# An RWKV-style recurrence followed by a multiplicative feed-forward: the order of every engine's instructions comes from the kernel's own list schedule

## The chip, the cores and the metric

The kernel runs on one core of one Trainium2 chip. The metric is the device time of one execution in microseconds (us). The time before is the median of three runs, 225.25 us (224.19 to 225.88).

## The reference

For each of 4 batches and 8 heads a state of 48 by 48 runs over 768 steps; the outputs, 3072 tokens of 384, then go through a feed-forward with a product of two projections.

```python
def _attn_ref(r, k, v, w, u):
    ...
    for t in range(S):
        kt, vt, rt, wt = (k[:, :, t], v[:, :, t], r[:, :, t], w[:, :, t])
        cur = np.einsum('bhd,bhe->bhde', u[None] * kt, vt)
        y[:, :, t] = np.einsum('bhd,bhde->bhe', rt, state + cur)
        state = wt[:, :, :, None] * state + np.einsum('bhd,bhe->bhde', kt, vt)
def _moe_ref(x, w1, w2, w3, w_out):
    return ((x @ w1) * (x @ w2) @ w3) @ w_out
```

Shapes: r, k, v, w are 4 x 8 x 768 x 48 float32; w1 and w2 are 384 x 1024, w3 is 1024 x 1024, w_out is 1024 x 384.

## The kernel before

**Units.** The sequence is cut into chunks of 128 steps. A unit is one chunk of one batch with all 8 heads: 24 units, n = 0 to 23, six for each batch, which hand a state on from unit to unit. `load(n)` (L102) issues four transfers on SyncE (SP) for a unit: w, k, r, v, each 128 partitions of eight rows of 192 bytes. Eight units' buffers exist, so `load(n + 8)` stands behind `att(n)` in the program (L304).

**Attention of a unit.** This is a chain that goes back and forth between engines: ScalarE (ACT) takes the logarithm of w (L121); TensorE (PE) forms the cumulative sums `cs` (L145); ACT takes the exponential (L146); VectorE (DVE) multiplies k and r by it into `krt` (L148); PE transposes `krt` in eight steps into `tr` (L152); ACT copies `tr` to `trs` (L155); PE forms the scores `mps` (L185); DVE masks them in two halves, `mbf` (L188); PE forms `y` from the state and the masked scores (L225, L230); DVE adds `yd` (L235); PE transposes the result, `yt` (L238); ACT copies it into the block's `xT` (L243). Beside it PE forms the state's increment `kv` and a column of decays (L194, L198), ACT takes an exponential (`pc`, L202), DVE adds the state (L207) and scales it (L215), and GpSimd (POOL) writes the state as a block-diagonal operand (`sbd`, L211). POOL also casts v (L124) and forms u times k times r (`uk`, L158, L159); DVE reduces that to `dsum` (L167) and POOL multiplies it with v (`yd`, L169).

**Feed-forward.** Units are gathered in blocks of 2, 2, 4, 4, 4, 4, 2, 2. For a block, `ffn_ab` (L249) runs for eight slices of 128 columns: three matmuls with w1 into `a_ps`, three with w2 into `b_ps`, an ACT copy of `a_ps` (L263), a DVE product into `abT` (L264). w3 and w_out are multiplied once into `w34`: `w34_transpose` (L275) transposes w3 in eight groups of eight, `w34_mul` (L281) runs eight groups of eight matmuls into `pm`. `ffn_out` (L266) runs eight matmuls for each unit, an ACT copy, and the store on SP.

**Weights.** `load_w` (L129) issues w1 and w2 on POOL in the middle of unit 1 (L161), w3 and w_out in the middle of unit 3 (L164). POOL issues nothing else of transfers.

**The order.** The program is written as a list of feed-forward parts with a cost in us each (L310 to L328): blocks 0 and 1 of `ffn_ab`, the transposes of w3, the products `w34`, the two blocks of `ffn_out`, then block by block. Before each part, units are emitted as long as `nxt < lead + done / every` with lead 3 and every 4.1 (L330). The framework then puts the instructions of each engine in an order of its own by that program order, by data dependence, by free buffers and by its own durations; only the four weight issues are pinned to their place. Once built, each engine works through its instructions strictly in that order.

Of the kernel before, what the change touches and what calls it, by code (L numbers as in the profile page):

```python
# [7 lines left out]
F32 = mybir.dt.float32  # L8
BF = mybir.dt.bfloat16
Alu = mybir.AluOpType  # L10
Act = mybir.ActivationFunctionType


@with_exitstack
def kernel(
# [26 lines left out]
    NTOK = B * S  # L42
# [17 lines left out]
    ps_ffn = ctx.enter_context(tc.tile_pool(name="ps_ffn", bufs=3, space=bass.MemoryType.PSUM))  # L60
    ps_att = ctx.enter_context(tc.tile_pool(name="ps_att", bufs=2, space=bass.MemoryType.PSUM))
# [30 lines left out]
    for t in lw_st:  # L92
        nc.vector.memset(t.rearrange("p h d -> p (h d)").bitcast(F32), 0.0)
    for t in kr_st:
        nc.vector.memset(t.rearrange("p g h d -> p (g h d)").bitcast(F32), 0.0)
    for t in sb_st:
        nc.vector.memset(t.rearrange("p h d -> p (h d)").bitcast(F32), 0.0)


    ins = {}  # L100

    def load(n):  # L102
        b, c = divmod(n, NC)

        def src(ap):
            return ap[b, :, c * C:(c + 1) * C, :].rearrange("h t d -> t h d")

        w_in = inp.tile([C, H, D], F32, tag="w_in", name="w_in")
        kr_in = inp.tile([C, 2, H, D], F32, tag="kr_in", name="kr_in")
        v_in = inp.tile([C, H, D], F32, tag="v_in", name="v_in")  # L110
        nc.sync.dma_start(w_in, src(w))  # L111
        nc.sync.dma_start(kr_in[:, 0], src(k))  # L112
        nc.sync.dma_start(kr_in[:, 1], src(r))  # L113
        nc.sync.dma_start(v_in, src(v))  # L114
        ins[n] = (w_in, kr_in, v_in)

    vbs = {}

    def prep(n):
        lw = lw_st[n % NS]  # L120
        nc.scalar.activation(lw[:, :, 0:D], ins[n][0], Act.Ln)  # L121
        lws[n] = lw
        v_bf = work.tile([C, H, D], BF, tag="v_bf", bufs=3)
        nc.gpsimd.tensor_copy(v_bf, ins[n][2])  # L124
        vbs[n] = v_bf

    lws = {}

    def load_w(dst, ap):  # L129
        with tc.high_priority():  # L130
            d = nc.gpsimd.dma_start(dst, ap.rearrange("(i p) f -> p i f", p=P))
        tc.keep_in_program_order(d)

    state = {}

    def att_a(n):

        b, c = divmod(n, NC)
        lw = lws[n]
        v_bf = vbs[n]  # L140
        kr_in = ins[n][1]
        e_sb = work.tile([C, 2, H, D], F32, tag="e_sb")
        cs = ps_m.tile([C, 2, TB], F32, tag="m", name="cs")
        for j, lt in enumerate((LTn_incl, LT_strict)):
            nc.tensor.matmul(cs[:, j, 0:DM], lhsT=lt, rhs=lw[:, :, 0:D], start=True, stop=True)  # L145
        nc.scalar.activation(e_sb.rearrange("t j h d -> t j (h d)"), cs[:, :, 0:DM], Act.Exp)  # L146
        krt = kr_st[n % NS]
        nc.vector.tensor_mul(krt[:, :, :, 0:D], kr_in, e_sb)  # L148
        tr = ps_att.tile([C, 2, HP, C], BF, tag="att")
        for j in range(2):  # L150
            for p in range(HP):
                nc.tensor.transpose(tr[:, j, p, :],  # L152
                                    krt[:, j, 2 * p:2 * p + 2, :].rearrange("t h d -> t (h d)"), I128)
        trs = work.tile([C, 2, HP, C], BF, tag="trs")
        nc.scalar.copy(trs, tr)  # L155

        uk = work.tile([C, H, D], F32, tag="uk")
        nc.gpsimd.tensor_mul(uk, kr_in[:, 0], u_bc)  # L158
        nc.gpsimd.tensor_mul(uk, uk, kr_in[:, 1])  # L159
        if n == 1:  # L160
            load_w(w1_bf, moe_w1)  # L161
            load_w(w2_bf, moe_w2)
        if n == 3:
            load_w(w3_bf, moe_w3)  # L164
            load_w(wo_bf, moe_w_out)
        dsum = work.tile([C, H], F32, tag="dsum")
        nc.vector.reduce_sum(dsum, uk, axis=mybir.AxisListType.X)  # L167
        yd = work.tile([C, H, D], BF, tag="yd")
        nc.gpsimd.tensor_mul(yd, v_bf, dsum[:, :, None].to_broadcast([C, H, D]))  # L169
        state[n] = (krt, trs, yd)  # L170

    prev = {}

    def att_b(n):

        b, c = divmod(n, NC)
        lw = lws.pop(n)
        v_bf = vbs.pop(n)
        krt, trs, yd = state.pop(n)
        mbf = work.tile([C, 2, HP, C], BF, tag="mbf")  # L180
        mps = ps_m.tile([C, 2, HP, C], F32, tag="m", name="mps")
        for p in range(HP):
            for q in range(2):
                o = q * DP
                nc.tensor.matmul(mps[:, q, p, :], lhsT=trs[o:o + D, 0, p, :],  # L185
                                 rhs=trs[o:o + D, 1, p, :], start=True, stop=True)
        for q in range(2):
            nc.vector.tensor_mul(mbf[:, q], mps[:, q], mask)  # L188

        if c < NC - 1:  # L190
            kv = ps_att.tile([C, HP, D + 1], F32, tag="att")
# [5 lines left out]
            for p in range(HP):
                nc.tensor.matmul(kv[:, p, D:D + 1],  # L198
                                 lhsT=lw[:, 2 * p:2 * p + 2, :].rearrange("t h d -> t (h d)"),
                                 rhs=ones_c, start=True, stop=True)  # L200
            pc = work.tile([C, HP], F32, tag="pc")
            nc.scalar.activation(pc[:, :, None], kv[:, :, D:D + 1], Act.Exp)  # L202
            ts_ = work.tile([C, HP, D], F32, tag="tsum")
            if c == 0:
                nc.vector.tensor_copy(ts_, kv[:, :, 0:D])
            else:
                nc.vector.tensor_add(ts_, prev[b][0], kv[:, :, 0:D])  # L207
            s_bd = sb_st[n % NS]
            for q in range(2):
                o = q * DP  # L210
                nc.gpsimd.tensor_mul(s_bd[o:o + DP, :, q * D:(q + 1) * D], ts_[o:o + DP],  # L211
                                     pc[o:o + DP, :, None].to_broadcast([DP, HP, D]))
            s_f = work.tile([C, HP, D], F32, tag="s_f")
            if c < NC - 2:
                nc.vector.tensor_mul(s_f, ts_, pc[:, :, None].to_broadcast([C, HP, D]))  # L215
            nxt = (s_f, s_bd)
        else:
            nxt = None

        y = ps_y.tile([C, H, D], F32, tag="y")  # L220
        first = True
        if c > 0:
            s_bd = prev[b][1]
            for p in range(HP):
                nc.tensor.matmul(y[:, 2 * p:2 * p + 2, :], lhsT=trs[:, 1, p, :], rhs=s_bd[:, p, :],  # L225
                                 start=first, stop=False)
                first = False
        for p in range(HP):
            for q in range(2):
                nc.tensor.matmul(y[:, 2 * p + q, :], lhsT=mbf[:, q, p, :], rhs=v_bf[:, 2 * p + q, :],  # L230
                                 start=first, stop=(p == HP - 1 and q == 1))
                first = False
        prev[b] = nxt
        y_bf = work.tile([C, DM], BF, tag="y_bf")
        nc.vector.tensor_add(y_bf.rearrange("t (h e) -> t h e", h=H), y, yd)  # L235
        yt = ps_att.tile([C, DI, C], BF, tag="att")
        for di in range(DI):
            nc.tensor.transpose(yt[:, di, :], y_bf[:, di * P:(di + 1) * P], I128)  # L238
# [127 lines left out]
```

## Time and profile before

| quantity | value |
|---|---|
| median of three runs | 225.25 us (224.19 to 225.88) |
| the profiled execution's own time | 225.09 us |
| its span, first to last instruction | 223.4 us |
| PE busy | 176.8 us, 79% of the span |
| DVE busy | 133.1 us, 60% |
| POOL busy | 115.4 us, 52% |
| ACT busy | 108.9 us, 49% |
| bytes moved | 28.54 MB in 106342 packets, of which 100304 are under 512 bytes |

The span is that of one profiled execution; its time is 1.7 us more than the span, and 0.16 us under the median. "Busy" of PE is the union of its matmuls' records, whose ends are modelled, so that it also holds the last matmul's way through the array ahead of a pause. L numbers are lines of the kernel before. A row of a timeline gives the start, the length of the group, the engine and line, the operation, the number of instructions, and in brackets the idle time of the engine ahead of it with what ended it.

### The profile page before, as it was taken

To read this page: it belongs to the slowest core of one execution; us is meant where nothing else is said; L and a number is where in the kernel's file an instruction comes from. 1 tells how busy PE (TensorE), PEld (TensorE's weight loads), DVE (VectorE), ACT (ScalarE), POOL (GpSimd) and SP (SyncE) were. 2 spreads that over 40 slices of the span, in tenths; PEclk is the share of its full clock that TensorE was granted. 3 is DMA by queue.
4 is the path that set the end of the run, shared out by engine and by line. 5 is a ranking of instruction groups with operands and counts; after the bars stand their busy time and mean duration, and the time that the engine had idled before them with its cause. 6 is when DMAs were issued, how large, how long until landed. Compare 5 with 4: busy or idle time off the path is not lost.

```text
span 223.4 us, 4564 instructions
## 1 busy us (share of the span) xinstructions
PE 176.8 (79%) x1720; PEld 103.5 (46%) x1720; DVE 133.1 (60%) x238; ACT 108.9 (49%) x213; POOL 115.4 (52%) x152
## 2 busy tenths in 40 slices
PE   1044169805898898987899879998999999999993
PEld 0033136603576555553355534455545544557771
DVE  5174055426579964456878458773897657853360
ACT  3222234603462374636565566567566566544441
POOL 4598265136997588767636775767363332100000
PEclk9999999975899999999999999999999999999999
DMA  7999999999999999996449987611000110002101
GB/s 130 197 167 200 202 182 193 199 190 183 195 190 168 195 170 202 177 213 107 109 95 197 203 187 165 113 36 74 35 3 0 72 72 0 3 37 106 38 37 70
DMA packets 106342, 28.54 MB, mean 128 GB/s; under 512 B 100304, under 2 KB 104528, under 8 KB 106320
## 3 DMA queue, kind: packets, MB, share of 16 engines
q1 hardware_dynamic: 103440, 23.80, 58.7%
q0 software_dynamic: 2880, 4.46, 11.4%
q8 instruction: 13, 0.21, 0.4%
q14 instruction: 9, 0.07, 0.1%
HBM read 27.98 MB, written 4.72 MB: 146 GB/s over the span
## 4 chain that ended last, share of the span: by engine, by line
PE 39%; SPq 14%; DMA 14%; POOL 13%; DVE 8%; issue 7%; ACT 3%; POOLq 0%; DVEq 0%; ACTq 0%
DMA v_in<-in_v_dram 9%; PE b_ps L260 9%; PE a_ps L256 8%; PE o_ps L269 7%; DVE krt L148 7%; SPq L113 6%; PE tr L152 5%; POOL yd L169 4%; DMA kr_in<-in_k_dram 4%; SPq L114 3%; POOL sbd L211 3%; SPq L112 3%; SPq L111 2%; POOL uk L159 2%; PE mps L185 2%
## 5 line engine op out<-in xcount | busy, mean ns | idle before, releaser
L264 DVE TENSOR_TENSOR abT<-a_sb,b_ps 128x256 bf16<-128x256 f32 (+1 forms) x64 | 35.0, 549 | 23.2 <-ACT a_sb L263 11.8
L256 PE MATMUL a_ps<-xT,w_bf 128*128 128x256 bf16 (+1 forms) x192 | 45.6, 333 | 3.6 <-ACT xT L243 2.4
L260 PE MATMUL b_ps<-xT,w_bf 128*128 128x256 bf16 (+1 forms) x192 | 45.4, 332 | 2.3 <-ACT a_sb L263 1.8
L263 ACT COPY a_sb<-a_ps 128x256 f32<-128x256 f32 (+1 forms) x64 | 30.6, 481 | 23.2 <-PE a_ps L256 22.5
L158 POOL TENSOR_TENSOR uk<-kr_in,u_bc 128x384 f32<-128x384 f32 x24 | 29.3, 1221 | 23.5 <-DMA kr_in<-in_k_dram 11.8
L155 ACT COPY trs<-tr 128x1024 bf16<-128x1024 bf16 x24 | 24.3, 1012 | 25.6 <-PE tr L152 25.5
L269 PE MATMUL o_ps<-w,abT 128*128 128x384 bf16 x192 | 36.5, 325 | 0.0
L148 DVE TENSOR_TENSOR krt<-kr_in,e_sb 128x768 bf16<-128x768 f32 x24 | 27.2, 1132 | 12.0 <-ACT e_sb L146 12.0
L188 DVE TENSOR_TENSOR mbf<-mps,mask 128x512 bf16<-128x512 f32 x48 | 30.8, 682 | 3.1 <-PE mps L185 2.8
L146 ACT ACTIVATE e_sb<-cs 128x768 f32<-128x768 f32 x24 | 19.5, 811 | 21.0 <-PE cs L145 20.9
L152 PE MATMUL tr<-I,krt 128*128 128x128 bf16 x192 | 16.6, 235 | 13.4 <-DVE krt L148 13.2
L159 POOL TENSOR_TENSOR uk<-uk,kr_in 128x384 f32<-128x384 f32 x24 | 26.3, 1096 | 1.6
L167 DVE TENSOR_REDUCE dsum<-uk 128x8 f32<-128x384 f32 x24 | 13.2, 549 | 23.2 <-POOL uk L159 14.6
L256 PEld LDWEIGHTS <-w_bf 128*128 128x128 bf16 x192 | 18.1, 100 | 11.5 <-issue 2.7
L124 POOL CAST v_bf<-v_in 128x384 bf16<-128x384 f32 x24 | 12.0, 505 | 22.3 <-DMA v_in<-in_v_dram 7.5
L152 PEld LDWEIGHTS <-krt 128*128 128x128 bf16 x192 | 12.6, 106 | 22.6 <-DVE krt L148 22.3
L260 PEld LDWEIGHTS <-w_bf 128*128 128x128 bf16 x192 | 18.2, 99 | 10.4 <-issue 3.0
L169 POOL TENSOR_TENSOR yd<-v_bf,dsum 128x384 bf16<-128x384 bf16 x24 | 20.6, 860 | 4.0 <-DVE y_bf L235 2.8
L121 ACT ACTIVATE lw<-w_in 128x384 bf16<-128x384 f32 x24 | 12.7, 529 | 19.9 <-DMA w_in<-in_w_dram 19.9
L269 PEld LDWEIGHTS <-abT 128*128 128x128 bf16 x192 | 17.3, 97 | 9.7
L230 PE MATMUL y<-v_bf,mbf 128*128 128x48 bf16 x192 | 13.3, 189 | 9.9 <-DVE mbf L188 9.6
L230 PEld LDWEIGHTS <-mbf 128*128 128x128 bf16 x192 | 9.4, 98 | 22.1 <-DVE mbf L188 20.3
(99 smaller groups left out, 204.5 us busy)
## 6 DMA issues: line engine op xcount, KB each, us to landing
w_in<-in_w_dram SPq DMA_DIRECT2D x24, 192.0 KB, 4.5
kr_in<-in_k_dram SPq DMA_DIRECT2D x24, 192.0 KB, 4.5
kr_in<-in_r_dram SPq DMA_DIRECT2D x24, 192.0 KB, 4.6
v_in<-in_v_dram SPq DMA_DIRECT2D x24, 192.0 KB, 4.5
out_dram<-o_sb SPq DMA_DIRECT2D x24, 192.0 KB, 1.9
w_bf<-in_moe_w_dram POOLq DMA_DIRECT2D x1, 2048.0 KB, 15.6
w_bf<-in_moe_w_dram POOLq DMA_DIRECT2D x2, 768.0 KB, 9.8
wo_bf<-in_moe_w_out_dram POOLq DMA_DIRECT2D x1, 768.0 KB, 20.1
```

The lines of the kernel that those rows point to most:

```text
L148: nc.vector.tensor_mul(krt[:, :, :, 0:D], kr_in, e_sb)
L152: nc.tensor.transpose(tr[:, j, p, :], krt[:, j, 2 * p:2 * p + 2, :].rearrange("t h d -> t (h d)"), I128)
L155: nc.scalar.copy(trs, tr)
L158: nc.gpsimd.tensor_mul(uk, kr_in[:, 0], u_bc)
L159: nc.gpsimd.tensor_mul(uk, uk, kr_in[:, 1])
L169: nc.gpsimd.tensor_mul(yd, v_bf, dsum[:, :, None].to_broadcast([C, H, D]))
L188: nc.vector.tensor_mul(mbf[:, q], mps[:, q], mask)
L256: nc.tensor.matmul(a_ps[:, 0:T], lhsT=w1_bf[:, di, fi * P:(fi + 1) * P], rhs=x[:, di, 0:T], start=(di == 0), stop=(di == DI - 1))
L260: nc.tensor.matmul(b_ps[:, 0:T], lhsT=w2_bf[:, di, fi * P:(fi + 1) * P], rhs=x[:, di, 0:T], start=(di == 0), stop=(di == DI - 1))
L263: nc.scalar.copy(a_sb[:, 0:T], a_ps[:, 0:T])
L264: nc.vector.tensor_mul(abts[j][:, fi, 0:T], a_sb[:, 0:T], b_ps[:, 0:T])
L269: nc.tensor.matmul(o_ps, lhsT=abts[j][:, fi, t * P:(t + 1) * P], rhs=w34[:, fi, :], start=(fi == 0), stop=(fi == FI - 1))
```

## The change

Nothing that an engine computes is taken away, added, or given to another engine. A class `Plan` collects steps: a name, an engine, a length in us, the steps that it needs, buffers that it takes and frees, a rank. `_pass` then walks in time: for each engine it finds the steps that could start first, takes of these the one of lowest rank, and so fixes an order; `run` repeats this until the windows in which weights move stay as they were, and emits the steps in that order. Every instruction is wrapped in `keep_in_program_order`, so the framework leaves it in place. Ranks are the order in which the steps are added, which is the program order of before, with lead 3 and every 4.1 kept; stores and weight issues have rank -1.

The steps' lengths are constants. A transfer of a unit's input counts 1024 rows; rows pass at 1000 per us, but at 85 per us while weights move, at most eight transfers are under way, and each lands 1.9 us after its last row. w1 and w2 need the landing of unit 0's r, w3 and w_out that of unit 3's v. These needs only enter the planned time: no instruction waits for them.

Smaller edits: three buffers instead of two for `yd`, `a_sb` and `o_sb`; in `y` the matmuls on the first masked half come ahead of those on the second; the constants `I128` and `mask` are written by POOL at the start of the program and `ones_c` last of DVE's memsets; loads of all 24 units are steps of their own, held back only by their buffers.

```diff
+class Plan:
+    HOP = 0.06
...
+    def _pass(self, windows):
...
+            for n in ready:
+                s = left[n]
+                t = eng_free.get(s["eng"], 0.0)
+                for d in s["needs"]:
+                    t = max(t, end[d] + (self.HOP if self.steps[d]["eng"] != s["eng"] else 0.0))
...
+                if s["rows"] and len(ring) >= 8:
+                    t = max(t, ring[-8])
+                best.setdefault(s["eng"], []).append((t, s["rank"], n))
...
+            for e, c in best.items():
+                t0 = min(c)[0]
+                picks.append(min((max(t, t0), r, n) for t, r, n in c if t <= t0 + 1e-9))
+            t, _, n = min(picks)
...
+                    rate = 85.0 if w else 1000.0
...
+                end[n] = at + 1.9
...
+            elif s["big"]:
+                at = max(t + 2.0, big_free)
+                big_free = at + s["big"]
+                new_windows.append((at, big_free))
+                end[n] = big_free + 1.5
...
+class InOrder:
...
+            return self.tc.keep_in_program_order(f(*a, **k))
...
+    pe, act, dve, pool, sp = (InOrder(tc, e) for e in (nc.tensor, nc.scalar, nc.vector, nc.gpsimd, nc.sync))
...
+    plan.buffers(w_in=NIN, kr_in=NIN, v_in=NIN, lw=NS, krt=NS, sbd=NS, v_bf=3, e_sb=2, uk=2, ds=2, yd=3,
+                 trs=2, mbf=2, pc=2, ts=2, s_f=2, y_bf=2, a_sb=3, o_sb=3, xT=3, abT=3, f=3, t=2, m=1, y=1)
...
+        plan.add(f"ld_w{n}", "SP", 0.06, ld_w, take=["w_in"], rows=1024)
...
+    def load_w(name, dst, ap, size, needs):
+        plan.add(name, "POOL", 0.9, lambda: pool.dma_start(dst, ap.rearrange("(i p) f -> p i f", p=P)),
+                 needs=needs, big=size, rank=-1)
...
+        A(f"ln{n}", "ACT", 0.46, ln, needs=[f"ld_w{n}"], take=["lw"], free=[f"ld_w{n}"])
+        A(f"cs{n}", "PE", 0.33, cs, needs=[f"ln{n}"], take=["m"], lag=0.2, free=[] if not last else [f"ln{n}"])
+        A(f"ex{n}", "ACT", 0.75, ex, needs=[f"cs{n}"], take=["e_sb"], free=[f"cs{n}"])
+        A(f"krt{n}", "DVE", 1.1, krt, needs=[f"ex{n}", f"ld_k{n}", f"ld_r{n}"], take=["krt"],
+          free=[f"ex{n}", f"ld_k{n}"])
...
+        A(f"uk1{n}", "POOL", 1.05, uk1, needs=[f"ld_k{n}", "ld_u"], take=["uk"])
...
+        A(f"ds{n}", "DVE", 0.5, ds, needs=[f"uk2{n}"], take=["ds"], free=[f"uk1{n}"])
+        A(f"yd{n}", "POOL", 0.82, yd, needs=[f"ds{n}", f"vb{n}"], take=["yd"], free=[f"ds{n}"])
...
+        A(f"a{j}.{fi}", "PE", 0.65 * s, lambda: half("a", w1_bf), needs=xs + ["w1"], take=["f"], lag=0.2)
...
+        A(f"o{j}.{t_}", "PE", 1.3, o, needs=[f"ab{j}.{fi}" for fi in range(FI)] + [f"wc{fi}" for fi in range(FI)],
+          take=["f"], lag=0.2, free=[f"ab{j}.0"] if t_ == hi - lo - 1 else [])
...
+    load_w("w1", w1_bf, moe_w1, 4.25, ["ld_r0"])
+    load_w("w2", w2_bf, moe_w2, 4.25, ["w1"])
+    load_w("w3", w3_bf, moe_w3, 11.4, ["w2", "ld_v3"])
+    load_w("wo", wo_bf, moe_w_out, 5.0, ["w3"])
+    plan.steps["w2"]["needs"], plan.steps["wo"]["needs"] = ["ld_r0"], ["ld_v3"]
...
+    plan.run()
```

## Rows read from the trace of the kernel before

**Rows 1.** The page's first lines: span, and busy time of the engines.
```profile
span 223.4 us, 4564 instructions
PE 176.8 (79%) x1720; PEld 103.5 (46%) x1720; DVE 133.1 (60%) x238; ACT 108.9 (49%) x213; POOL 115.4 (52%) x152
```
**Rows 2.** Windows: start:end, length, busy us of PE, PEld, DVE, ACT, POOL, PEclk, DMA share.
```profile
0.00:50.50 50.50, 20.85 (x213) 13.53 (x213) 21.75 (x44) 15.56 (x30) 26.88 (x42) 0.97 1.10 185
50.50:72.20 21.70, 17.28 (x195) 12.44 (x196) 15.40 (x31) 9.61 (x20) 17.51 (x22) 0.84 1.14 183
51.00:58.00 7.00, 5.05 (x44) 3.40 (x45) 2.74 (x6) 3.12 (x7) 5.58 (x7) 0.53 0.93 181
72.20:92.00 19.80, 17.93 (x197) 10.82 (x194) 12.96 (x23) 10.60 (x21) 15.01 (x17) 1.00 1.19 189
92.00:150.00 58.00, 52.92 (x516) 27.47 (x515) 40.55 (x70) 33.80 (x64) 37.58 (x45) 1.00 0.78 142
150.00:199.50 49.50, 47.63 (x457) 24.91 (x456) 35.72 (x59) 29.68 (x54) 18.39 (x28) 1.00 0.09 33
199.50:219.70 20.20, 20.20 (x151) 14.38 (x148) 6.74 (x16) 9.19 (x24) 0.00 (x0) 1.00 0.16 60
```
**Rows 3.** Timeline of ACT, DVE and PE: three stops, and the first `ffn_ab` of block 0.
```profile
25.81 0.52 ACT L121 ACTIVATE lw<-w_in 128x384 bf16<-128x384 f32 x1 [4.01 <-DMA w_in<-in_w_dram]
...
32.28 0.80 PE L256 MATMUL a_ps<-xT,w_bf 128*128 128x256 bf16 x3 [0.57 <-ACT xT L243]
...
48.72 0.55 DVE L167 TENSOR_REDUCE dsum<-uk 128x8 f32<-128x384 f32 x1 [6.95 <-POOL uk L159]
...
50.52 0.22 PE L230 MATMUL y<-v_bf,mbf 128*128 128x48 bf16 x1 [6.31 <-DVE mbf L188]
```
**Rows 4.** Timeline of POOL: the weights' issues.
```profile
12.96 1.70 POOL L131 DMA_DIRECT2D w_bf<-in_moe_w_dram  x2
...
30.05 0.94 POOL L131 DMA_DIRECT2D w_bf<-in_moe_w_dram  x1
```
**Rows 5.** The page's transfers: KB each, median us from issue to landing.
```profile
w_bf<-in_moe_w_dram POOLq DMA_DIRECT2D x1, 2048.0 KB, 15.6
wo_bf<-in_moe_w_out_dram POOLq DMA_DIRECT2D x1, 768.0 KB, 20.1
```
**Rows 6.** Timeline of SP: two input issues while w1 and w2 move, and one after.
```profile
15.03 7.12 SPq L113 DMA_DIRECT2D kr_in<-in_r_dram  x1
22.19 3.15 SPq L114 DMA_DIRECT2D v_in<-in_v_dram  x1
...
26.31 0.98 SPq L112 DMA_DIRECT2D kr_in<-in_k_dram  x1
```
**Rows 7.** Timeline of PE: one unit's attention between other matmuls, read by starts.
```profile
89.02 0.62 PE L152 MATMUL tr<-I,krt 128*128 128x128 bf16 x8 [0.56 <-DVE krt L148]
...
89.92 0.97 PE L284 MATMUL pm<-wo_bf,w3T 128*128 128x384 bf16 x5
90.83 0.40 PE L185 MATMUL mps<-trs 48*128 48x128 bf16 x8
...
91.34 0.98 PE L269 MATMUL o_ps<-w,abT 128*128 128x384 bf16 x5
...
92.94 0.34 PE L230 MATMUL y<-v_bf,mbf 128*128 128x48 bf16 x7
...
93.44 0.65 PE L269 MATMUL o_ps<-w,abT 128*128 128x384 bf16 x3
```
**Rows 8.** The chain that ended last: start, us, what (feed-forward matmuls).
```profile
156.37 0.65 PE b_ps L260 x3
...
199.54 3.58 PE o_ps L269 x22
```
**Rows 9.** One tile's and one line's view: lengths min/median/max in ns; waits.
```profile
L148 DVE TENSOR_TENSOR krt<-kr_in,e_sb x24: 947/1092/1655, 10.5 to 193.4; 128x768 bf16<-128x768 f32 x24
...
  DVE dsum L167: 8.5, 8
```

More of the change, by code (lines that the diff above doesn't have):

```diff
@@ L119, in prep @@
[L119 to L136, printed above, removed]
-        b, c = divmod(n, NC)
[L139 to L150, printed above, removed]
-            for p in range(HP):
[L152 to L182, printed above, removed]
+        def ld_w():
+            T["w_in", n] = inp.tile([C, H, D], F32, tag="w_in", name="w_in")
+            sp.dma_start(T["w_in", n], src(w))
+        def ld_k():
+            T["kr_in", n] = inp.tile([C, 2, H, D], F32, tag="kr_in", name="kr_in")
+            sp.dma_start(T["kr_in", n][:, 0], src(k))
@@ L183, in att_b @@
             for q in range(2):
                 o = q * DP
[L185 to L191, printed above, removed]
+                pool.tensor_mul(t[o:o + DP, :, q * D:(q + 1) * D], T["ts", n][o:o + DP],
+                                T["pc", n][o:o + DP, :, None].to_broadcast([DP, HP, D]))
@@ L197, in att_b @@
[L197 to L207, printed above, removed]
@@ L220, in att_b @@
[L220 to L232, printed above, removed]
@@ L233, in att_b @@
[L233 to L238, printed above, removed]
+                    o = q * DP
+                    pe.matmul(t[:, q, p, :], lhsT=trs_[o:o + D, 0, p, :], rhs=trs_[o:o + D, 1, p, :],
+                              start=True, stop=True)
@@ new lines, in mb, with y @@
+        def mb(q):
+            if q == 0:
+                T["mb", n] = work.tile([C, 2, HP, C], BF, tag="mbf", name="mbf")
+            dve.tensor_mul(T["mb", n][:, q], T["m", n][:, q], mask)
+        def y():
+            t = T["y", n] = ps_y.tile([C, H, D], F32, tag="y", name="y")
+            first = True
+            if c > 0:
+                for p in range(HP):
+                    pe.matmul(t[:, 2 * p:2 * p + 2, :], lhsT=T["trs", n][:, 1, p, :],
+                              rhs=T["sbd", n - 1][:, p, :], start=first, stop=False)
+                    first = False
+            for q in range(2):
+                for p in range(HP):
+                    pe.matmul(t[:, 2 * p + q, :], lhsT=T["mb", n][:, q, p, :], rhs=T["vb", n][:, 2 * p + q, :],
+                              start=first, stop=(p == HP - 1 and q == 1))
+                    first = False
@@ new lines, in att @@
+        A(f"ex{n}", "ACT", 0.75, ex, needs=[f"cs{n}"], take=["e_sb"], free=[f"cs{n}"])
+        A(f"krt{n}", "DVE", 1.1, krt, needs=[f"ex{n}", f"ld_k{n}", f"ld_r{n}"], take=["krt"],
+          free=[f"ex{n}", f"ld_k{n}"])
+        A(f"tr{n}", "PE", 0.46, tr, needs=[f"krt{n}"], take=["t"], lag=0.2, free=[] if not last else [f"krt{n}"])
+        A(f"trs{n}", "ACT", 0.95, trs, needs=[f"tr{n}"], take=["trs"], free=[f"tr{n}"])
+        A(f"vb{n}", "POOL", 0.5, vb, needs=[f"ld_v{n}"], take=["v_bf"], free=[f"ld_v{n}"])
@@ new lines, in att @@
+        if not last:
+            A(f"kv{n}", "PE", 0.42, kv, needs=[f"krt{n}", f"vb{n}"], take=["t"], lag=0.2,
+              free=[f"krt{n}", f"ln{n}"])
+            A(f"ts{n}", "DVE", 0.32, ts, needs=[f"kv{n}"] + ([f"s_f{n - 1}"] if c else []), take=["ts"],
+              free=[f"kv{n}"] + ([f"s_f{n - 1}"] if c else []))
+            A(f"pc{n}", "ACT", 0.13, pc, needs=[f"kv{n}"], take=["pc"], free=[f"kv{n}"])
+            two = c < NC - 2
+            A(f"sbd{n}", "POOL", 1.15, sbd, needs=[f"ts{n}", f"pc{n}"], take=["sbd"],
+              free=[f"ts{n}", f"pc{n}"])
+            if two:
+                A(f"s_f{n}", "DVE", 0.32, s_f, needs=[f"ts{n}", f"pc{n}"], take=["s_f"],
+                  free=[f"ts{n}", f"pc{n}"])
@@ L247 @@
+        if n != lo:
+            plan.steps[f"xt{n}"]["needs"].append(f"xt{lo}")
     out3 = out.rearrange("(n t) o -> n t o", t=P)
     def ffn_ab(j, fi):
[L250 to L257 removed]
@@ new lines, in ffn_ab, with half, a_cp @@
+        N = (hi - lo) * C
+        s = N / 512
+        def half(nm, w_):
+            t = T[nm, j, fi] = ps_f.tile([P, TB], F32, tag="f", name=nm)
+            for di in range(DI):
+                pe.matmul(t[:, 0:N], lhsT=w_[:, di, fi * P:(fi + 1) * P], rhs=T["xT", j][:, di, 0:N],
+                          start=(di == 0), stop=(di == DI - 1))
+        def a_cp():
+            t = T["as", j, fi] = work.tile([P, TB], F32, tag="a_sb", name="a_sb", bufs=3)
+            act.copy(t[:, 0:N], T["a", j, fi][:, 0:N])
@@ new lines, in ffn_ab, with ffn_out, o, os @@
+        A(f"as{j}.{fi}", "ACT", 0.1 + 0.43 * s, a_cp, needs=[f"a{j}.{fi}"], take=["a_sb"], free=[f"a{j}.{fi}"])
+        A(f"ab{j}.{fi}", "DVE", 0.1 + 0.53 * s, mul,
+          needs=[f"as{j}.{fi}", f"b{j}.{fi}"] + ([f"ab{j}.0"] if fi else []), take=[] if fi else ["abT"],
+          free=[f"as{j}.{fi}", f"b{j}.{fi}"])
+    def ffn_out(j, t_):
+        lo, hi = BLOCKS[j]
+        def o():
+            t = T["o", j, t_] = ps_f.tile([P, DM], F32, tag="f", name="o_ps")
+            for fi in range(FI):
+                pe.matmul(t, lhsT=T["abT", j][:, fi, t_ * P:(t_ + 1) * P], rhs=w34[:, fi, :],
+                          start=(fi == 0), stop=(fi == FI - 1))
+        def os():
+            t = T["os", j, t_] = work.tile([P, DM], F32, tag="o_sb", name="o_sb", bufs=3)
+            act.copy(t, T["o", j, t_])
+        def st():
+            sp.dma_start(out3[lo + t_], T["os", j, t_])
+        A = plan.add
+        A(f"o{j}.{t_}", "PE", 1.3, o, needs=[f"ab{j}.{fi}" for fi in range(FI)] + [f"wc{fi}" for fi in range(FI)],
+          take=["f"], lag=0.2, free=[f"ab{j}.0"] if t_ == hi - lo - 1 else [])
+        A(f"os{j}.{t_}", "ACT", 0.43, os, needs=[f"o{j}.{t_}"], take=["o_sb"], free=[f"o{j}.{t_}"])
+        A(f"st{j}.{t_}", "SP", 0.06, st, needs=[f"os{j}.{t_}"], free=[f"os{j}.{t_}"], rows=300, rank=-1)
@@ new lines, in w34_mul, with wm @@
+    def w34_mul(fi):
+        def wm():
+            t = T["wm", fi] = ps_f.tile([P, DM], F32, tag="f", name="wm")
+            for gi in range(FI):
+                pe.matmul(t, lhsT=w3T[:, gi, fi * P:(fi + 1) * P], rhs=wo_bf[:, gi, :],
+                          start=(gi == 0), stop=(gi == FI - 1))
+        plan.add(f"wm{fi}", "PE", 1.3, wm, needs=["wo"] + [f"w3T{gi}" for gi in range(FI)], take=["f"], lag=0.2)
+        plan.add(f"wc{fi}", "ACT", 0.43, lambda: act.copy(w34[:, fi, :], T["wm", fi]), needs=[f"wm{fi}"],
+                 free=[f"wm{fi}"])
@@ L325 @@
     add_out(1)
[L326 removed]
+    for j in range(2, NB):
         add_ab(j)
```

312 lines of the change are left out of this document (219 added, 93 removed).

## The prediction

> **What bounds the kernel now.** I read the page's first lines first, then the windows, then the timelines of the stops, and the chain only to get prices. The reader should see PE busy for 176.8 of 223.4 us, and no other engine above 60% of the span [rows 1]. So PE is the engine to follow, and the question is where its other 46.6 us lie. The windows answer it [rows 2]: up to 50.5 us PE is busy 20.85 us, from 50.5 to 72.2 us 17.28 of 21.7, from 72.2 to 199.5 us 118.5 of 127.3, and in the last stretch all the time. Thus 34 of the idle 47 us lie before 72.2 us, 9 in the long middle, and 3.7 us at the end are the last copy and store.
>
> The early idle time is in part the input's: nothing can be transposed before unit 0 has landed, and w3 and w_out are issued at 30.05 us and take 15.6 and 20.1 us [rows 4, 5], so they land at about 45.6 and 51 us. But part of it comes from the order [rows 3]. At 21.8 us ACT takes up the logarithm of a unit whose w has not landed, and stands 4.0 us with a finished `tr` behind it. At 41.8 us DVE stands 6.95 us at a `dsum` whose inputs crawl in beside w3, and behind it the masked scores of an older unit, for which PE waits 6.31 us until 50.52. Then PE runs at a granted clock of 0.53, about the lower of its two levels (1.2 of 2.4 GHz), from 51 to 58 us [rows 2]. Block 1 of `ffn_ab`, whose inputs had long landed, comes only after that, and w3's transposes, possible from 46 us, end near 72.2 us, where I set a boundary of the windows.
>
> Busy time flatters the middle, as it counts the matmuls' way through the array. So I price PE's work by the distance between starts. Of one unit's attention [rows 7]: `tr` with `kv` 0.90 (89.02 to 89.92), `mps` with the state's part of `y` 0.51 (90.83 to 91.34), the rest of `y` with `cs` 0.50 (92.94 to 93.44), and an estimate of 0.2 for `yt` (three transposes, where the eight of `tr` take 0.62): 2.1 us. Three matmuls of 512 columns take 0.65 and 22 of `o_ps` 3.58 us, so 0.163 each [rows 8]; a slice of 256 columns is put at half, 0.325. The whole program is then 24 x 2.1 = 50.4 for attention, 64 x 0.65 = 41.6 and 64 x 0.325 = 20.8 for the two projections, 192 x 0.163 = 31.3 for `ffn_out`, 64 x 0.163 = 10.4 for `w34_mul`, and 8 x 0.62 = 5.0 for w3's transposes: 159.5 us. By 72.2 us the kernel before has done six units (12.6), blocks 0 and 1 of `ffn_ab` (10.4) and w3's transposes (5.0), 28.0 in all; the other 131.5 us take it 147.5 us, to 219.7. That is a pace of 0.89, although PE looks busy 0.94 of that time.
>
> **The change, part by part.** No instruction is added, removed or given to another engine, so every term is time that PE stands.
>
> The start. The plan gives w1 and w2 to POOL at the landing of unit 0's r, but the issue doesn't wait for that landing: on POOL's queue only the constants stand ahead of it. It will go out at 3 to 6 us instead of 12.96 [rows 4]. While w1 and w2 move, two input issues take 10.3 us, where 0.98 each is usual [rows 6], so the window costs the input 8.3 us. It now falls on units 0 and 1 instead of units 3 and 4: unit 1 will be whole at about 20 us, later than before, but unit 3 at the same time as before, 28 us, as the bytes ahead of it are the same. Block 0 can start when unit 1 has gone through the chain, about 8 us by its parts, at 28; before, it started at 32.3, when its `xT` came [rows 3]. From outcome to outcome this part is worth 3 us lost (unit 0 late, and every in-order queue behind it) to 4 won; I take 2 won.
>
> 28 to 52 us. In this stretch PE has blocks 0 and 1 of `ffn_ab` (10.4), two units (4.2), and from 45 us w3's transposes (5.0): 19.6 us of work in 24, so it can be done if no queue stands. The plan knows that input crawls beside w3, puts the steps of units 4 and 5 where their rows land, and leaves nothing old behind them. So at about 52 us it has 4 x 2.1 + 10.4 + 5.0 = 23.8 us of work behind it and 135.7 ahead. The kernel before reaches blocks 0, 1 and the transposes at 72.2, with two units more (4.2 us). Net, the early part is worth 20.2 - 4.2 / 0.89 = 15.5 us; at worst nothing of it, if other stops take their place.
>
> What is late next: after 52 us there are `w34_mul` (10.4), `ffn_out` of two blocks (four units, 5.2) and units 4 to 7 (8.4), 24 us, and unit 7 lands near 60 (units 6 and 7, four issues each at 0.98, from 51 on [rows 6]), so input is not the bound again. PE needs 2.1 + 3.9 = 6 us a unit, the input 4.
>
> The middle. Here `dsum` waits 8.5 us in eight waits for POOL's `yd` to release a buffer [rows 9], and `krt` stands behind it on DVE. The third `yd` buffer and the chosen order remove that; DVE's load allows it, as it is busy 40.55 of 58 us [rows 2]. Bounds for the pace: 0.89 as before, and 0.95, about what the busy share already shows there. Fixed lengths can't be right for all instances: `krt` runs from 947 to 1655 ns [rows 9] where the plan says 1.1, and whoever comes late holds up a whole queue. So I take 0.92, nearer to the row of before than to a full PE: 135.7 / 0.92 = 147.5 us.
>
> The end. The last copy, store and landing stay: 223.4 - 219.7 = 3.7 us, and 1.7 us from span to time. The third `o_sb` and `a_sb` buffers and the order of `y`'s halves I put at nothing: PE is full where they act, and half of `mbf`, 0.68 us, is the most that a unit's chain gains.
>
> Sum, against the execution of 225.09 us: 52 + 147.5 + 3.7 + 1.7 = 204.9, or 205 us. That profiled execution is 0.16 us under the median of the three runs, so no correction is due.
>
> One rule speaks against the fixed order. `krt` reads two operands from SBUF while POOL multiplies on SBUF, and its longest run is 0.71 us over its shortest [rows 9]. The Trainium skill, page "SBUF — State Buffer", section "Who interferes with whom", says that such a VectorE instruction and a GpSimd instruction that reads SBUF exclude each other, and that the one issued second waits in full. The spread of `krt` agrees with it. A plan with one length for each step can't see who comes second.
>
> **The rivals.**
> The middle keeps its pace: only the early part comes, and the loops between DVE and POOL re-form. 52 + 135.7 / 0.89 = 204.5, and 5.4 more: 210 us. For it: ranks, lead and 4.1 are kept. Against it: the `yd` buffer and the order that put `dsum` ahead of `krt` change.
>
> No change: the early stops come back in other places. Unit 0's r arrives beside w1, the queues planned for 6 us stand until 15, block 0 starts at 32 as before, and in w3's window a step planned too early stops DVE once more. Then the state of 72.2 us is reached at 71 to 73, and the time is 223 to 227 us. For it: the plan's needs are no waits, so its first 15 us are wrong. Against it: PE has next to no other work then, and a queue whose head is merely late keeps its order.
>
> Slower: the fixed queues lose to the lengths that vary. If in each of the 20 units after 52 us a collision of `krt` with POOL stops PE for 1.0 us at the transposes, with no matmul put ahead of them as filler, 20 us come on top of the 210: 230 us. It decides from about 0.8 us a unit on. For it: `krt` alone varies by 0.71, and PE stands ahead of `tr` already. Against it: the framework's order of before was just as fixed when it ran, and lost less than that.
>
> **How the numbers follow.** Forecast 205 us (chance 0.62); pace kept, 210 (0.20); no change, 225 (0.06); slower, 230 (0.12). The low end is a pace of 0.95: 52 + 142.8 + 5.4 = 200, and 3 us off for an early part that is done at 49: 197. The high end takes in a pace of 0.89 with an early part worth little, up to the edge of no change: 222. About 1% is what a measurement of this kernel can tell from none; faster by more than that are the first two, 0.82, within it 0.06, slower 0.12.
>
> **What would show it.** Right, if in the changed profile the weight issues come at 3 to 6 us and again near 28; if w3's transposes end by 52 to 55 and PE has no idle piece over 3 us after 30; if the granted clock stays at full from 45 to 60; if DVE's `dsum` no longer waits for `yd`; and if PE's busy share from 55 us to the end is 0.95 or more. Wrong, if block 0 starts after 32 us, if DVE or POOL stand for several us beside w3's transfer as they do now, or if PE's waits for `krt` and for the masked scores come back after 72 us in larger pieces.

## The result, and the profile after

The changed kernel takes 201.1 us (median, 200.42 to 201.39), beside 224.98 for the kernel before on the same chip: a ratio of 0.8933, 95% interval 0.889 to 0.8976. The profiled execution took 201.36 us.

The page's first lines of the changed kernel, which answer to [rows 1]:

```profile
span 199.7 us, 4541 instructions
PE 168.0 (84%) x1708; PEld 107.3 (54%) x1720; DVE 133.4 (67%) x238; ACT 110.3 (55%) x213; POOL 117.5 (59%) x152
```

The busy time of DVE, ACT and POOL is the same within about 2 us. The span is shorter by 23.7 us: 14.9 of these are idle time of PE (46.6 us before, 31.7 now) and 8.8 are its busy time. PE's work is the same. That its busy time is lower likely comes from fewer matmuls at the lower clock or ahead of a pause; and 12 records of PE are missing from this trace (1708 of 1720), which lowers the count too. How much each makes is not shown.

The windows of the changed kernel (columns as in [rows 2]); 56.4 us is where w3's transposes end here, as 72.2 was before:

```profile
0.00:50.50 50.50, 27.26 (x306) 19.13 (x306) 27.05 (x57) 19.75 (x40) 32.06 (x47) 1.00 1.11 179
50.50:72.20 21.70, 20.84 (x240) 14.60 (x239) 17.85 (x30) 12.24 (x24) 15.52 (x19) 1.00 1.06 183
45.00:60.00 15.00, 14.54 (x182) 11.21 (x180) 12.27 (x23) 8.13 (x18) 6.53 (x9) 1.00 1.07 182
56.40:150.00 93.60, 89.28 (x914) 53.29 (x922) 76.07 (x125) 62.07 (x115) 77.20 (x93) 1.00 0.94 170
150.00:196.00 46.00, 45.57 (x412) 29.92 (x415) 25.35 (x49) 25.48 (x52) 6.76 (x10) 1.00 0.12 44
```

PE does 27.26 us of work by 50.5 us instead of 20.85, and from 45 to 60 us it is busy 14.54 of 15 us at the full granted clock, where it stood and then ran at 0.53 before. In the middle the busy share is 0.95, and DVE and POOL are both busy above 0.8 of the time (76 and 77 of 93.6 us); before, from 72.2 to 150 us, it was 0.69 and 0.68 [rows 2].

The first 57 us are not clean, though. Timelines of ACT, DVE and PE of the changed kernel, in the manner of [rows 3]:

```profile
18.38 0.52 ACT L136 ACTIVATE lw<-w_in 128x384 bf16<-128x384 f32 x1 [9.06 <-DMA w_in<-in_w_dram]
...
18.99 0.36 DVE L136 TENSOR_TENSOR s_f<-ts__198,pc 128x192 f32<-128x192 f32 x1 [9.80 <-ACT pc L136]
...
20.01 0.34 PE L136 MATMUL y<-v_bf,mbf 128*128 128x48 bf16 x4 [10.04 <-DVE mbf L136]
...
30.73 1.44 PE L136 MATMUL a<-xT,w_bf 128*128 128x256 bf16 x6 [0.74 <-ACT xT L136]
...
52.65 3.79 PE L136 MATMUL wt<-I,w_bf 128*128 128x128 bf16 x56
```

Here one reads a chain of three queue heads: ACT stands 9.06 us at unit 1's logarithm, whose w comes in beside w1; unit 0's decay `pc` is behind it on ACT, DVE waits for `pc` with unit 0's masked scores behind it, and PE waits 10.04 us for these. The first three rows are these heads. Block 0 starts at 30.73 us (32.28 before), and the transposes end at 56.4.

POOL's weight issues, and the two input issues on SP that stood while w1 and w2 moved:

```profile
3.53 1.71 POOL L136 DMA_DIRECT2D w_bf<-in_moe_w_dram  x2
...
32.10 0.94 POOL L136 DMA_DIRECT2D w_bf<-in_moe_w_dram  x1
```
```profile
5.68 9.22 SPq L136 DMA_DIRECT2D kr_in<-in_r_dram  x1
14.95 3.19 SPq L136 DMA_DIRECT2D v_in<-in_v_dram  x1
```

And the landings of w3 and w_out on the page, as in [rows 5]:

```profile
w_bf<-in_moe_w_dram POOLq DMA_DIRECT2D x1, 2048.0 KB, 15.4
...
wo_bf<-in_moe_w_out_dram POOLq DMA_DIRECT2D x1, 768.0 KB, 19.5
```

w1 and w2 go out at 3.53 us, 9.4 us earlier than before; w3 at 32.10, 2 us later than before, so that it lands at 47.5.

One view more, for [rows 9]: the line of `krt`, the waits at `dsum` (here `ds`), and PE's waits for `krt` (total us, times, longest), first in the kernel before from 72.2 us on, then here from 56.4 us on:

```profile
L136 DVE TENSOR_TENSOR krt<-kr_in,e_sb x24: 943/958/1715, 6.2 to 172.3; 128x768 bf16<-128x768 f32 x24
...
  DVE ds L136: 3.0, 2
```
```profile
PE tr L152 <- DVE krt L148: 6.2, 12, 1.2
```
```profile
PE tr L136 <- DVE krt L136: 1.5, 3, 0.8
```

DVE waits for POOL's `yd` twice, for 3.0 us, where it waited eight times, for 8.5; PE's waits for `krt` in the middle are down from 6.2 to 1.5 us.

### The profile page after: what moved, and what is told of

Its sections match the earlier page's. It is cut to its first block, busy times and chain, and to the rows that moved or that the text cites. A ratio compares the mean times of both kernels' runs of the same rounds, so it can differ in the third digit from the quotient of the medians.

```text
span 199.7 us, 4541 instructions
## 1 busy us (share of the span) xinstructions
PE 168.0 (84%) x1708; PEld 107.3 (54%) x1720; DVE 133.4 (67%) x238; ACT 110.3 (55%) x213; POOL 117.5 (59%) x152
## 4 chain that ended last, share of the span: by engine, by line
PE 54%; POOL 13%; DVE 10%; DMA 8%; issue 5%; ACT 5%; SPq 2%; POOLq 0%; ACTq 0%; DVEq 0%
PE b L136 13%; PE o_ps L136 13%; PE a L136 12%; DMA w_in<-in_w_dram 7%; POOL uk L136 6%; PE tr L136 4%; POOL sbd L136 3%; DVE mbf L136 3%; PE y L136 3%; PE m L136 3%; POOL yd L136 3%; PE cs L136 2%; PE kv L136 2%; DVE krt L136 2%; SPq L136 2%
## 5 line engine op out<-in xcount | busy, mean ns | idle before, releaser
L136 DVE TENSOR_TENSOR abT<-a_sb,b 128x256 bf16<-128x256 f32 (+1 forms) x64 | 34.1, 548 | 14.7 <-PE b L136 7.8
L136 PE MATMUL a<-xT,w_bf 128*128 128x256 bf16 (+1 forms) x189 | 38.8, 329 | 1.7 <-ACT xT L136 1.3
L136 PE MATMUL b<-xT,w_bf 128*128 128x256 bf16 (+1 forms) x183 | 38.9, 325 | 1.3 <-DVE abT L136 0.5
L136 ACT COPY a_sb<-a 128x256 f32<-128x256 f32 (+1 forms) x64 | 30.2, 481 | 16.8 <-PE a L136 14.6
L136 DVE TENSOR_TENSOR mbf<-m,mask 128x512 bf16<-128x512 f32 x48 | 31.6, 680 | 3.7 <-PE m L136 3.7
L136 POOL TENSOR_TENSOR yd<-v_bf,ds 128x384 bf16<-128x384 bf16 x24 | 23.5, 980 | 7.2 <-DVE ds L136 5.1
L136 PEld LDWEIGHTS <-krt 128*128 128x128 bf16 (+1 forms) x352 | 17.5, 108 | 13.0 <-DVE krt L136 7.1
L136 PEld LDWEIGHTS <-abT 128*128 128x128 bf16 x192 | 17.7, 97 | 10.9
L136 DVE TENSOR_REDUCE ds<-uk 128x8 f32<-128x384 f32 x24 | 13.1, 546 | 10.8 <-POOL uk L136 7.8
L136 ACT COPY o_sb<-o_ps 128x384 f32<-128x384 f32 x24 | 11.5, 478 | 15.4 <-PE o_ps L136 12.9
L136 DVE TENSOR_TENSOR y_bf<-y,yd 128x384 bf16<-128x384 f32 x24 | 13.2, 551 | 6.6 <-PE y L136 4.6
```

The source lines that it names most:

```text
L136: return self.tc.keep_in_program_order(f(*a, **k))
```

## The experiments

Times are medians; each ratio is to runs of the kernel before beside it. In five runs (without the weight windows, equal lengths, off by 20%, mean lengths, attention first) the plan has one more rule, left out of the diffs here: a unit's r is issued only behind its k. The changed kernel's SP issues k ahead of r in all 24 units without it.

**Two buffers again.**

```diff
-    ... yd=3, ... a_sb=3, o_sb=3
+    ... yd=2, ... a_sb=2, o_sb=2
```

> The changed kernel, with two buffers again instead of three for yd, a_sb and o_sb, in the pools and in the plan. If the order does the work (theory), the plan orders around the two buffers and the time stays within 3 us of the changed kernel's 201.1: 199 to 204 us. If the third buffers carry the better pace of the middle (rival), the pace falls back from 0.96 to about 0.89 of PE's priced work, and the time rises by about 10 us, to 209 to 213.

Measured: 202.03 us, ratio 0.8964 (0.8933 to 0.8995), against 0.8933 (0.889 to 0.8976) for the changed kernel. The intervals overlap: by the medians the third buffers are worth 0.9 us, which these runs can't tell from nothing.

**Three buffers in the kernel before.**

```diff
-        yd = work.tile([C, H, D], BF, tag="yd")
+        yd = work.tile([C, H, D], BF, tag="yd", bufs=3)
```
and the same for `a_sb` and `o_sb`.

> The kernel before, with three buffers instead of two for yd, a_sb and o_sb, and nothing else. If the order does the work (theory), the framework's order keeps its early stops: 222 to 226 us. If the waits of dsum for yd's buffer (8.5 us) set the pace of the middle (rival), these go and the time falls by 5 to 10 us, to 215 to 220.

Measured: 226.61 us, ratio 1.0044 (1.0012 to 1.0075). Together the two runs rule out the buffers as the cause of the better pace. The waits at `dsum` in this run's trace, as in [rows 9]:

```profile
  DVE dsum L167: 9.3, 6
```

They are not shorter than the 8.5 us of before, and the program says why: `dsum` writes a buffer of its own, of which there are two, and must wait until `yd` of two units earlier has read it. A third buffer for `yd` doesn't free that one.

**Early weights in the kernel before.** w1 and w2 are issued ahead of the first unit's work on POOL.

```diff
-        if n == 1:
-            load_w(w1_bf, moe_w1)
-            load_w(w2_bf, moe_w2)
...
+    load_w(w1_bf, moe_w1)
+    load_w(w2_bf, moe_w2)
     def att(n):
```

> The kernel before, with the issues of w1 and w2 moved from the middle of unit 1 to the front of POOL's program, as they lie in the changed kernel in effect. If the earlier issue isn't what brings the gain (theory), the time stays at 222 to 228 us. If the weights' earlier arrival is a good part of it (rival), block 0 starts at 28 us or earlier and the time falls by 4 us or more, to 214 to 221.

Measured: 223.43 us, ratio 0.9934 (0.9899 to 0.997). The timelines of ACT and PE show what is lost at the start:

```profile
17.38 0.52 ACT L121 ACTIVATE lw<-w_in 128x384 bf16<-128x384 f32 x1 [12.88 <-DMA w_in<-in_w_dram]
...
19.65 1.04 PE L152 MATMUL tr<-I,krt 128*128 128x128 bf16 x8 [14.30 <-DVE krt L148]
...
37.38 0.80 PE L253 MATMUL a_ps<-xT,w_bf 128*128 128x256 bf16 x3 [0.57 <-ACT xT L240]
```

ACT stands 12.88 us at unit 1's logarithm with unit 0's exponential behind it, a queue head once more, so unit 0 is transposed only at 19.65 us. Block 0 starts 5 us later than before, yet the time is 1.5 us shorter. The earlier weights by themselves are not the gain.

**Pins without a plan.** The kernel before, with every instruction kept in the order in which the program is written.

```diff
+    class InOrder:
...
+                return tc.keep_in_program_order(f(*a, **k))
```

> The kernel before, with every instruction pinned to the program order as it is written (a whole unit's attention, then feed-forward parts), without a plan. If what counts is which order is fixed (theory), every engine now stands through a unit's chain of some 8 us again and again, with feed-forward parts only between units: over 260 us. If fixing the order as such were enough, because the framework's reordering is what hurts (rival), 200 to 225 us.

Measured: 362.06 us, ratio 1.6065 (1.5921 to 1.6208). The page:

```profile
span 358.0 us, 4569 instructions
## 1 busy us (share of the span) xinstructions
PE 232.3 (65%) x1720; PEld 133.2 (37%) x1720; DVE 132.4 (37%) x238; ACT 116.0 (32%) x213; POOL 107.6 (30%) x152
```

DVE has the same work in 1.6 times the span. So pinning as such loses much; what wins is which order is pinned.

**The plan without the weight windows.** Rows keep their 1000 per us while weights move.

```diff
-                    rate = 85.0 if w else 1000.0
+                    rate = 1000.0
```

> The changed kernel, but the plan lets input rows pass at 1000 per us while weights move, too (85 before); lengths, buffers and ranks as they are. If the plan's knowledge of the weight windows does part of the work (theory), steps of units 4 to 6 are put ahead of older work and stand beside w3's transfer, as DVE did for 6.95 us in the kernel before: 205 to 212 us, with an idle piece of PE over 3 us between 35 and 55 us. If that knowledge is worth nothing, as PE has no other work in those stretches anyway (rival), 200 to 203 us.

Measured: 217.33 us, ratio 0.964 (0.9598 to 0.9683): 16 us of the 24 are gone, more than I had expected at the most. Timelines of ACT and PE, and one window:

```profile
54.17 0.52 ACT L138 ACTIVATE lw<-w_in 128x384 bf16<-128x384 f32 x1 [7.90 <-DMA w_in<-in_w_dram]
...
55.01 0.80 PE L138 MATMUL b<-xT,w_bf 128*128 128x256 bf16 x3 [6.38 <-ACT a_sb L138]
...
40.00:60.00 20.00, 8.75 (x79) 6.09 (x79) 7.76 (x15) 5.97 (x13) 7.44 (x11) 0.61 1.15 189
```

ACT takes up the logarithm of a unit whose w is held back beside w3, with a copy of a running `ffn_ab` behind it, and PE waits for that copy: 8.75 us of work in 20, at a granted clock of 0.61. This is the stop of the kernel before, in another place. PE did have other work, so the rival falls.

**One length for all steps.** Transfers, dependences, buffers and ranks stay; every step on PE, ACT, DVE and POOL counts 0.7 us.

```diff
-            eng_free[s["eng"]] = t + s["length"]
+            length = 0.7 if s["eng"] not in ("SP",) and not s["big"] else s["length"]
+            eng_free[s["eng"]] = t + length
```

> The changed kernel, but the plan gives every step on PE, ACT, DVE and POOL the same length, 0.7 us (weight issues excepted); dependences, buffers, ranks and the transfers' rates stay. If the measured lengths matter (theory), the plan misjudges which engine is late, and PE waits more in the middle: 205 to 215 us. If dependences, buffers and ranks suffice (rival), 200 to 204 us.

Measured: 224.05 us, ratio 0.9959 (0.9928 to 0.999). All of the gain is gone, far beyond either expectation. The same window of the changed kernel and of this one:

```profile
52.00:150.00 98.00, 93.62 (x977) 56.95 (x983) 80.16 (x131) 63.20 (x118) 78.65 (x95) 1.00 0.94 171
```
```profile
52.00:150.00 98.00, 83.91 (x840) 52.20 (x845) 69.05 (x114) 52.95 (x100) 67.43 (x82) 0.94 0.95 165
```

PE, DVE, ACT and POOL all do 10 to 11 us less in 98 us, and PE is busy 0.86 of it, so none of the four is full. From 30 us on PE waits 14 times for `krt`, 10.9 us in all, where the changed kernel waits 3 times and 1.5 us; no single wait is over 2.0 us.

**Lengths off by up to 20%**, each step by its own fixed factor.

```diff
+        if eng != "SP" and not big:
+            length *= 0.8 + 0.4 * (len(self.steps) * 0.618034 % 1.0)
```

> The changed kernel, but every planned length on PE, ACT, DVE and POOL (weight issues excepted) is multiplied by a fixed factor between 0.8 and 1.2 that differs from step to step. Equal lengths of 0.7 us had cost 23 us. If that was because the sums of an engine's load came out wrong, and not because single steps did (theory), errors that cancel over a few steps cost little: 201 to 206 us. If the fixed order needs each length right (rival), it loses a large part of the gain: 210 to 222 us.

Measured: 201.29 us, ratio 0.8928 (0.8893 to 0.8963). Nothing is lost.

**Each engine's mean length.** The loads of the engines are right in sum, single steps are not.

```diff
+        for e in ("PE", "ACT", "DVE", "POOL"):
+            mine = [s for s in self.steps.values() if s["eng"] == e and not s["big"]]
+            mean = sum(s["length"] for s in mine) / len(mine)
+            for s in mine:
+                s["length"] = mean
```

> The changed kernel, but in the plan each step of an engine has that engine's mean length (PE 0.513, ACT 0.498, DVE 0.566, POOL 0.906 us), so that the sums of the engines' loads are right and single steps are not. One length of 0.7 for all engines, which put PE's sum at 216 instead of 158 us and POOL's at 81 instead of 105, had cost 23 us; errors of up to 20% that cancel had cost nothing. If the sums are what the plan needs (theory), 201 to 206 us. If it also needs to know which steps of an engine are long, as ffn_out with 1.3 and the state's column with 0.13 (rival), 212 us or more.

Measured: 213.08 us, ratio 0.9404 (0.9324 to 0.9483), which is the rival's range and not the theory's. The window from 52 to 150 us lies between the two above:

```profile
52.00:150.00 98.00, 88.94 (x920) 53.76 (x919) 71.26 (x121) 57.69 (x109) 72.46 (x88) 0.98 1.00 172
```

So both count: of the 23 us that one length for all had cost, right sums bring back 11, and 12 come from knowing which steps are long and which are short. An error of a fifth in a step is forgiven; taking PE's shortest step, 0.18 us, and its longest, 1.3, for the same is not.

**Attention ranked first.**

```diff
-    lead, every = 3, 4.1
+    lead, every = 24, 4.1
```

> The changed kernel with lead 24 instead of 3, so that every step of attention ranks ahead of every step of the feed-forward. If the rank decides little, since a step is taken when it can start and buffers hold attention back (theory), 200 to 204 us. If the ranks of before, with lead 3 and every 4.1, carry a good part of the pace (rival), attention takes DVE and POOL from the running blocks and leaves a tail of feed-forward alone: 206 to 215 us.

Measured: 200.15 us, ratio 0.8883 (0.8842 to 0.8924), overlapping with the changed kernel's. The rank decides little here.

**The true start.** The plan is told when each engine is free of its set-up, and that w1 and w2 go out at once.

```diff
-        end, eng_free, taken, owner, released = {}, {}, {}, {}, {}
+        end, eng_free, taken, owner, released = {}, dict(POOL=3.5, DVE=4.0, ACT=2.1, SP=0.8), {}, {}, {}
...
-    load_w("w1", w1_bf, moe_w1, 4.25, ["ld_r0"])
+    load_w("w1", w1_bf, moe_w1, 4.25, [])
```

> The changed kernel, with the plan told the true start: the engines free at 3.5 (POOL), 4.0 (DVE), 2.1 (ACT) and 0.8 us (SP), and w1 and w2 without needs, as they go out in fact at 3.5 us. If the 10 us for which PE waits on unit 0's masked scores (9.97 to 20.01) delay what follows (theory), ACT takes unit 0's decay ahead of unit 1's logarithm, block 0 starts 1 to 2 us earlier than 30.7, w3 is issued 1 to 3 us earlier than 32.1, and the time falls to 197 to 200 us. If unit 1's rows set block 0 in any case (rival), 200 to 202 us.

Measured: six runs in two groups, one at 199.8 us and five from 205.86 to 207.15, so no ratio is given. The profile is of the second group; timelines of POOL, DVE and PE:

```profile
29.43 0.94 POOL L136 DMA_DIRECT2D w_bf<-in_moe_w_dram  x1
...
46.69 0.55 DVE L136 TENSOR_REDUCE ds<-uk 128x8 f32<-128x384 f32 x1 [6.24 <-POOL uk L136]
...
48.16 1.03 PE L136 MATMUL tr<-I,krt 128*128 128x128 bf16 x8 [5.60 <-DVE krt L136]
```

The first stop did go: unit 0's scores are used at 10.84 us, block 0 starts at 27.82, and w3 is issued 2.7 us earlier. But now unit 4's rows fall beside w3 instead of ahead of it, and DVE stands at that unit's reduction just as in [rows 3]. No trace was kept of the run at 199.8 us, so that it lacks this stop is a guess.

**The true start, with w3 after unit 4's r.**

```diff
-    load_w("w3", w3_bf, moe_w3, 11.4, ["w2", "ld_v3"])
+    load_w("w3", w3_bf, moe_w3, 11.4, ["w2", "ld_r4"])
```

> The kernel of the true start, with w3 and w_out planned at the landing of unit 4's r instead of unit 3's v, about three input transfers later. In the true start's profile w3 was issued at 29.43 us instead of 32.10, unit 4's rows came in beside it, and DVE stood 6.24 us at unit 4's reduction. If that transfer's side of the window is what splits its six runs into 199.8 and 205.9 to 207.2 (theory), all runs now lie together at 198 to 201 us, with no PE stop over 3 us between 30 and 60 us. If the true start itself is at fault (rival), the 206 us stay.

Measured: 199.22 us, 198.43 to 199.51 in six runs, ratio 0.8825 (0.8795 to 0.8854), against 0.8933 (0.889 to 0.8976). The intervals don't overlap, though the two were not run side by side; its median is the lowest of all. Timelines of POOL and PE:

```profile
36.02 0.94 POOL L136 DMA_DIRECT2D w_bf<-in_moe_w_dram  x1
...
51.90 1.07 PE L136 MATMUL wt<-I,w_bf 128*128 128x128 bf16 x16 [0.40 <-DMA w_bf<-in_moe_w_dram]
...
57.29 2.77 PE L136 MATMUL wm<-wo_bf,w3T 128*128 128x384 bf16 x16 [0.67 <-DMA wo_bf<-in_moe_w_out_dram]
```

w3 goes out 3.9 us later than in the changed kernel, and PE has enough other work until then: it waits 0.40 us for w3 and 0.67 for w_out. The two groups of runs have become one, which is what the theory of the transfer's side of the window asked for; the six runs were on another chip than those of the true start, though.

**Weights after unit 1.** As the true start, with w1 and w2 planned at the landing of unit 1's r.

```diff
-    load_w("w1", w1_bf, moe_w1, 4.25, [])
+    load_w("w1", w1_bf, moe_w1, 4.25, ["ld_r1"])
```

> The kernel of the true start, with w1 and w2 planned at the landing of unit 1's r instead of at the start, which puts their issue behind unit 0's and part of unit 1's work on POOL, near 11 us (y also needs the cast v, and a also needs w2, in the plan). Input ahead of w3 is the same in bytes. If block 0 waits for unit 1's rows, which now land ahead of w1 and w2 (theory), it starts at 21 to 25 us instead of 30.7, blocks 0 and 1 are done by 44 us, and the time falls to 194 to 198 us. If w3's landing near 50 us sets what follows (rival), PE only stands later, and the time is 199 to 202 us.

Measured: 199.55 us, ratio 0.8871 (0.8833 to 0.8908). Timeline of PE:

```profile
23.25 1.44 PE L136 MATMUL a<-xT,w_bf 128*128 128x256 bf16 x6 [0.57 <-ACT xT L136]
...
47.77 4.40 PE L136 MATMUL wt<-I,w_bf 128*128 128x128 bf16 x64 [0.65 <-DMA w_bf<-in_moe_w_dram]
...
53.05 2.77 PE L136 MATMUL wm<-wo_bf,w3T 128*128 128x384 bf16 x16 [0.88 <-DMA wo_bf<-in_moe_w_out_dram]
```

Block 0 does start 7.5 us earlier, as the theory had it, but the time falls by only 1.5 us by the medians, and the intervals overlap. Blocks 0 and 1 are done before w3 has landed, and PE waits 0.65 us for w3 and 0.88 for w_out. w3's transposes end at 52.2 us instead of 56.4, again with five units done; where the rest of that lead is lost was not followed. In the time the rival is right, in the start of block 0 the theory.

## Why the prediction was right or wrong

The direction, the size and the mechanism held: 205 us was forecast with 197 to 222 around it, and 201.1 was measured. By its own terms, against the execution of 201.36 us:

**The early part was over-sized.** I had w3's transposes ending at 52 us with four units done, and 15.5 us won. They end at 56.4, with five units done (PE's transposes of the sixth come right behind). Against 72.2 us with six units that is 15.8 us less 2.1 / 0.89 for one unit, 13.4 us. What failed is the step on the weights' issue. That the plan's needs are no waits, and that w1 and w2 go out between 3 and 6 us, was right (3.53). The window cost the input 10.5 us (9.22 and 3.19, where 0.98 each is usual), not 8.3. But I let this delay only unit 0 and its followers by up to 3 us, and took w3's issue for 28 us. In fact the plan had put unit 1's logarithm ahead of unit 0's decay, three queues stood 9 to 10 us, POOL's work slid, and w3 went out at 32.10. The run with the true start shows what the stop is worth: without it, w3's issue comes 2.7 us earlier and block 0 2.9 us earlier. "Block 0 at 28" thus was the true start's value (27.82), not this kernel's.

**The middle was under-sized.** The priced work left at 56.4 us is 159.5 less five units (10.5), blocks 0 and 1 (10.4) and w3's transposes (5.0): 133.6 us. PE's last matmul ends at 196.0, so this takes 139.6 us, a pace of 0.957, above both bounds. I took 0.92 from bounds of 0.89 and 0.95, "nearer to the row of before", because fixed lengths can't follow `krt`'s spread. That reason is the step that failed. In the changed kernel itself `krt` runs from 943 to 1715 ns, and PE waits for it only 1.5 us in the middle; and planned lengths that are off by up to 20% cost nothing. It may be that a step late by some tenths of a us meets a PE queue with other work in it; that was not tried by itself. At the pace of before (131.5 / 147.5 = 0.8915) the same work would take 149.8 us, so the middle won 10.2 us, where I had put 4.7.

The two errors go opposite ways, 2.1 us too much and 5.5 too little, so that they cancel in part, and that much of the closeness is luck: 13.4 + 10.2 = 23.6 us won, beside the 23.7 between the two profiled executions; forecast were 15.5 + 4.7 = 20.2. The end cost 3.7 us and the way from span to time 1.7, as taken.

**The buffers.** "The third `yd` buffer and the chosen order remove that": the order does, and the buffer has no part in it. I misread [rows 9]: what `dsum` waits for is its own buffer, which `yd` reads, not a buffer of `yd`. With the third buffer in the kernel before, DVE waits 9.3 us in six waits; in the changed kernel 3.0 in two; with two buffers again 1.5 in two. I put the other two buffers at nothing, which stands.

**The smaller edits.** The order of `y`'s halves, the constants on POOL and the loads freed from their place in the program were not tried by themselves. They stand in the run with equal lengths too, where about 1 us of the gain is left. So with a poor order they win next to nothing; what they add to a good one is not shown.

**The signs.** Held: the first weight issue (3.53 us), no idle piece of PE over 3 us after 30 us (the longest wait is 0.8), the full clock, and PE's busy share, 0.97 from 56.4 us to its end. Missed: w3 goes out at 32.10 us and not near 28, its transposes end at 56.4 and not by 55, and `dsum` still waits for `yd`, though only 3.0 us.

**The clock.** Full from 45 to 60 us, as forecast; where a stop came back (the plan without windows), so did time at the lower level: 0.61 in the mean from 40 to 60 us.

**The rivals.** "The middle keeps its pace" (210) fell by the pace. "No change" described a real thing, the queues planned for 6 us that stand until 15 (until 20, in fact), but PE had next to no other work then, as said against it. Its mechanism came back in the plan without windows (217.33 us). With equal lengths its time came back, 224, but by many small waits and not by the early stops. "Slower" fell: DVE and POOL take up 0.8 of the middle, and PE's waits for `krt` shrink from 6.2 to 1.5 us.

**The rule on the shared port.** The Trainium skill, page "SBUF — State Buffer", section "Who interferes with whom", has the one issued second wait. `krt` still spreads from 943 to 1715 ns, but its median fell from 1092 to 958, while POOL's `yd` rose from 860 to 980 ns in the mean and the cast of v from 505 to 573 (their medians stay: 830 and 832, 504 and 504, so a few long ones make it). That fits a changed sequence of who comes second; which pair blocked which was not tried.

## What to carry to other kernels

When engines work through fixed queues, look first for a queue head that waits on a transfer with older work behind it: a plan that knows how slow small-row input gets beside a large weight transfer was worth 16 of 24 us here. This list schedule did not need exact lengths: up to 20% off cost nothing, while one length for each engine cost 12 us and one for all 23. The true start and the true moment of each transfer are worth less here, some 2 us when both are right (199.22 beside 201.1); but the true start alone made five of six runs slower, 205.86 to 207.15 us, and in the traced one unit 4's rows lie beside w3. Pinning an order without such a plan can lose far more than it wins.

## What was not expected of the hardware

One and the same program, that of the true start, took 199.8 us once and 205.86 to 207.15 five times. In the traced run of the second group unit 4's rows lie beside w3's transfer; with w3 issued behind them six runs lay within 1.1 us. That the side of the transfer decides between the groups is the likely reading, but the run at 199.8 us has no trace to show it. And the same two weight transfers held the input up by different amounts: the two issues that met them stood 9.22 and 3.19 us when the weights went out at 3.53 us, and 7.12 and 3.15 when they went out at 12.96 [rows 6]. Why is open.
